# Three small moves in the attention and Fourier phase: tiny copies to GpSimd, later roundings, a priority for a head's low parts

## The chip, the cores and the metric

The kernel runs on one core of one Trainium2 chip. The metric is the time of one execution on the device, in microseconds (us); the core's five instruction streams are TensorE (PE, with its weight loads as PEld), VectorE (DVE), ScalarE (ACT), GpSimd (POOL) and SyncE (SP, which here issues DMAs only). Each engine runs its own instructions in the order in which they stand in its stream, and waits at an instruction until what that needs is there.

## What is computed

The reference chains three parts on four batches of 576 positions and 512 features:

```python
def _attn_ref(q, k, v, f):                       # 4 batches, 8 heads, 576 x 64
    scores = scale * np.matmul(q, k.transpose(0, 1, 3, 2))
    cum = np.cumsum(np.log(np.clip(f, 0.0001, 1.0)), axis=-1)
    decay = cum[:, :, :, None] - cum[:, :, None, :]
    scores = np.where(causal, -1000000000.0, scores + decay)
    ...
    return np.matmul(attn, v)                    # attn: softmax of scores

def _moe_ref(x, w_ch1, w_ch2):
    mixed = np.real(np.fft.fft(np.fft.fft(x, axis=1), axis=2))
    u = x + mixed
    un = (u - mu) / np.sqrt(var + 1e-06)
    return u + np.maximum(un @ w_ch1, 0.0) @ w_ch2

def _moe2_ref(x, w_theta, w_tok_r, w_tok_i, w_ch):
    theta = x @ w_theta
    zr, zi = x * np.cos(theta), x * np.sin(theta)
    y = np.einsum('ts,bsd->btd', w_tok_r, zr) + np.einsum('ts,bsd->btd', w_tok_i, zi)
    u = x + y
    return u + np.maximum(u @ w_ch, 0.0)
```

Products are made in a 32-bit format with fewer mantissa bits. Where that would lose too much, a number is kept as a **high** part (rounded to the format) and a **low** part (what the rounding left), and both are multiplied.

## The kernel before

**Three phases.** The first, up to about 280 us, does the attention of 32 heads, one after the other, and between their instructions the Fourier transform of each batch as soon as its heads are there. The second (to about 730 us) normalises and applies the two wide matrices of `_moe_ref`; the third is `_moe2_ref`. In the second phase from its first blocks on, and in the third, the order is written out; in the first the program hands its pieces to a scheduler, which orders each engine's stream by a priority (the order in which the pieces are written) and by its own estimate of when operands are ready. What it estimates is not measured; what it puts in a row stays in that row on the chip.

**A head** (`prep_units`, `score_units`). `raw` holds a head's keys and queries, twice over on the two halves of the partitions. ScalarE rounds all of it into `hi` (L205) and copies the rounded queries into `q2` (L207; `q_99` and `q_100` by the head's parity). GpSimd makes the two low parts: of the queries into the lower half of `hi` (L209), of the keys into `kl` (L211), which the pair of heads shares and two further rows of which come from a DMA that GpSimd issues (L186). Five blocks of scores follow, 576 (in two pieces of 448 and 128), 512, 384, 256 and 128 columns wide: for each a product of the high parts (L230, which needs L205 and L209) and one with `kl` and `q2` (L231, which needs L207 and L211). VectorE scales and masks a block, finds its extreme and frees its bank (L239, tiles `P` and `mn`), ScalarE takes the exponential (L244), TensorE transposes (L269), VectorE and ScalarE fetch the result (L272, `PT`), TensorE multiplies by the values (L301). `wide` (L250, GpSimd) holds the reciprocal row sums, spread over a diagonal.

**A batch's Fourier transform** (`evac_pair`, `fft_units`). A pair of heads ends in the tile `X`, its mirror in `Y` (L327). GpSimd adds and subtracts them into `E` and `O` (L347, L350). `fft_units` then folds the time axis: `ee` from `E` (L379) and `oo` from `O` (L383), 128x574 elements each, on `two`, which is GpSimd for the first three batches and VectorE for the last. The two columns of `ee` that are their own mirror are copied by ScalarE (L380, 4 elements in a partition), which then rounds `ee` into `eh` (L381) and `oo` into `oh` (L384); the low parts `el` (L386) and `ol` (L388) go to `two`. TensorE's first transform reads `eh` and `el` (L408), `oh` and `ol` (L419). The same is done for a single row, `xx` (L372, its copy L373, `xh` L374, `xl` L375).

Three times, for the first three batches, this folding falls between two heads: near 100, 168 and 232 us. The text below calls these places **hole 0, hole 1 and hole 2**.

Of the kernel before, what the change touches and what calls it, by code (L numbers as in the profile page):

```python
# [13 lines left out]
ALU = mybir.AluOpType  # L14
# [37 lines left out]
def f(ap):  # L52
    return ap.bitcast(F32)


class Net:
    def __init__(self, ctx, tc, ins, out):
        self.ctx, self.tc, self.nc = ctx, tc, tc.nc
        self.i, self.out = ins, out
        nc = self.nc  # L60
        self.base = ctx.enter_context(tc.tile_pool(name="base", bufs=1))
        self.psa = ctx.enter_context(tc.tile_pool(name="psa", bufs=3, space=PSUM))
        self.psb = ctx.enter_context(tc.tile_pool(name="psb", bufs=3, space=PSUM))
        self.pt = ExitStack()
        self.pst = self.pt.enter_context(tc.tile_pool(name="pst", bufs=1, space=PSUM))
        self.nout = 0
        self.u = self.base.tile([128, 4, B * S], F32, name="u")
        self.ident = self.base.tile([128, 128], F32, name="ident")
        self.mean = self.base.tile([128, 128], F32, name="mean")
        nc.gpsimd.memset(self.mean, 1.0 / 512.0)  # L70
        self.eps = self.base.tile([128, 1], F32, name="eps")
        nc.gpsimd.memset(self.eps, 1e-6)
        self.un = {}
        self.stash = {}
        self.sdram = ctx.enter_context(tc.tile_pool(name="sdram", bufs=1, space=DRAM))

    def bank_a(self):
        return self.psa.tile([128, 512], F32, tag="a", name="pa")
# [116 lines left out]
    def prep_units(self, n, pair, raw, hd):  # L195
        nc = self.nc
        g = n % 2
        kl, q2 = pair["kl"], self.q2[g]
        hi = self.w2.tile([128, 2, S], F32R, tag="hi", name="hi")
        hd["hi"] = hi  # L200
        if n == 0:
            nc.scalar.copy(hi[:, 1], raw[:, 1])
            nc.scalar.copy(hi[:, 0], raw[:, 0])
        else:
            nc.scalar.copy(hi, raw)  # L205
        yield
        nc.scalar.copy(q2[0:64], raw[0:64, 1])  # L207
        lows = nc.vector if n == 0 else nc.gpsimd
        lows.tensor_tensor(hi[64:128, 1], raw[64:128, 1], f(hi[64:128, 1]), ALU.subtract)  # L209
        yield  # L210
        lows.tensor_tensor(kl[0:64, g], raw[0:64, 0], f(hi[0:64, 0]), ALU.subtract)  # L211
        yield

    def score_units(self, hd, g):
# [139 lines left out]
    def fft_units(self, b, E, O, rows):  # L354
        nc = self.nc
        w = self.c1
        x256 = self.x256
# [4 lines left out]
        two = nc.vector if b == B - 1 else nc.gpsimd  # L362
        ee = w.tile([128, 2, 290], F32, tag="ee", name="ee", bufs=1)
        oo = w.tile([128, 2, 288], F32, tag="oo", name="oo", bufs=1)
        xx = w.tile([1, 290], F32, tag="xx", name="xx", bufs=1)
        eh = w.tile([128, 2, 290], F32R, tag="eh", name="eh", bufs=1)
        el = w.tile([128, 2, 290], F32R, tag="el", name="el", bufs=1)
        oh = w.tile([128, 2, 288], F32R, tag="oh", name="oh", bufs=1)
# [1 line left out]
        xh, xl = self.xh, self.xl  # L370
        nc.gpsimd.memset(xx[:, 288:290], 0.0)
        nc.gpsimd.tensor_tensor(xx[:, 1:288], x256[:, 1:288], x256[:, 575:288:-1], ALU.add)  # L372
        nc.scalar.copy(xx[:, 0:289:288], x256[:, 0:289:288])  # L373
        nc.scalar.copy(xh[0:1], xx)  # L374
        nc.gpsimd.tensor_tensor(xl[0:1], xx, f(xh[0:1]), ALU.subtract)  # L375
        nc.gpsimd.memset(ee[:, :, 288:290], 0.0)
        nc.gpsimd.memset(oo[:, :, 286:288], 0.0)
        yield
        two.tensor_tensor(ee[:, :, 1:288], E[:, :, 1:288], E[:, :, 575:288:-1], ALU.add)  # L379
        nc.scalar.copy(ee[:, :, 0:289:288], E[:, :, 0:289:288])  # L380
        nc.scalar.copy(eh, ee)  # L381
        yield
        two.tensor_tensor(oo[:, :, 0:287], O[:, :, 1:288], O[:, :, 575:288:-1], ALU.subtract)  # L383
        nc.scalar.copy(oh, oo)  # L384
        yield
        two.tensor_tensor(el, ee, f(eh), ALU.subtract)  # L386
        yield
        two.tensor_tensor(ol, oo, f(oh), ALU.subtract)  # L388
        for _ in range(4):
# [799 lines left out]
```

## Time and profile before

| what | value |
|---|---|
| time, median of 3 runs | 970.92 us (970.60 to 971.12) |
| the profiled execution's own time | 972.97 us |
| its span | 971.2 us |
| TensorE busy in it | 906.7 us (93%) |
| ScalarE, GpSimd busy | 430.9 us, 337.4 us |

The span goes from the first to the last instruction that the profiler recorded; 1.8 us of the execution lie outside it. The profiled execution took 2.05 us more than the median of the runs. In every row of the trace the time at which an idle period ended stands with the instruction that began then, in brackets, with what released it. "Granted clock" is the clock that TensorE was given, as a share of the full 2.4 GHz; 0.50 is 1.2 GHz.

### The profile page before, as it was taken

To read this page: it belongs to the slowest core of one execution; us is meant where nothing else is said; L and a number is where in the kernel's file an instruction comes from. 1 tells how busy PE (TensorE), PEld (TensorE's weight loads), DVE (VectorE), ACT (ScalarE), POOL (GpSimd) and SP (SyncE) were. 2 spreads that over 40 slices of the span, in tenths; PEclk is the share of its full clock that TensorE was granted. 3 is DMA by queue.
4 is the path that set the end of the run, shared out by engine and by line. 5 is a ranking of instruction groups with operands and counts; after the bars stand their busy time and mean duration, and the time that the engine had idled before them with its cause. 6 is when DMAs were issued, how large, how long until landed. Compare 5 with 4: busy or idle time off the path is not lost.

```text
span 971.2 us, 15852 instructions
## 1 busy us (share of the span) xinstructions
PE 906.7 (93%) x5960; PEld 849.4 (87%) x5960; DVE 605.8 (62%) x1469; ACT 430.9 (44%) x1037; POOL 337.4 (35%) x381
## 2 busy tenths in 40 slices
PE   4899898997969999999999999999999999999998
PEld 3677676775748889999999999999999999999998
DVE  7666466474589796544765466536677765746554
ACT  5888677677553443212332222212334534525331
POOL 5776678677540334200000000000024644525330
PEclk9999899997999899999999999999999999999999
DMA  4643232222022121002214022333420000010001
GB/s 145 201 139 119 87 101 89 91 76 88 15 92 83 45 87 44 2 4 84 75 57 159 25 79 86 112 109 114 129 61 1 1 25 25 2 37 14 25 26 49
DMA packets 24336, 68.04 MB, mean 70 GB/s; under 512 B 3534, under 2 KB 6990, under 8 KB 24260
## 3 DMA queue, kind: packets, MB, share of 16 engines
q1 hardware_dynamic: 20420, 62.52, 19.9%
q0 software_dynamic: 3120, 3.33, 1.4%
q10 hardware_dynamic: 720, 1.18, 0.4%
q8 instruction: 47, 0.77, 0.3%
q14 instruction: 29, 0.24, 0.1%
HBM read 57.92 MB, written 9.07 MB: 69 GB/s over the span
## 4 chain that ended last, share of the span: by engine, by line
PE 58%; DVE 10%; ACT 3%; DMA 2%; issue 1%; POOL 1%; ACTq 0%; DVEq 0%; SPq 0%; POOLq 0%
PE pa L747 18%; PE pb L761 11%; PE po L761 8%; PE pb L968 5%; PE pa L979 4%; PE pa L932 4%; PE po L968 3%; DMA raw<-in_wf 1%; DVE kra L939 1%; DVE kra L956 1%; DVE kra L942 1%; DVE a L567 1%; DVE a L565 1%; PE pb L431 1%; DVE kra L941 1%
## 5 line engine op out<-in xcount | busy, mean ns | idle before, releaser
L747 PE MATMUL pa<-un,wf 128*128 128x384 f32 x1152 | 222.5, 341 | 5.3 <-ACT un L735 3.1
L747 PEld LDWEIGHTS pa<-un,wf 128*128 128x128 f32 x1152 | 204.1, 191 | 8.9 <-ACT un L735 4.2
L753 DVE SCALAR_TENSOR_TENSOR h<-pa,h 128x384 fp32r<-128x384 f32 x96 | 53.1, 556 | 145.0 <-ACT h L752 144.8
L761 PE MATMUL pb<-h,wf 128*128 128x384 f32 x660 | 134.9, 337 | 0.3 <-DVE u L769 0.3
L761 PEld LDWEIGHTS pb<-h,wf 128*128 128x128 f32 x660 | 116.6, 188 | 1.2 <-DVE u L769 1.0
L752 ACT ACTIVATE h<-pa 128x384 fp32r<-128x384 f32 x96 | 46.6, 489 | 151.6 <-PE pa L747 151.6
L244 ACT ACTIVATE P<-P,mn 128x512 f32<-128x512 f32 (+4 forms) x160 | 95.5, 600 | 37.7 <-DVE mn L239 37.3
L239 DVE CUSTOM_DVE_ANT_0 P<-pa,mask 128x448 f32<-128x448 f32 (+4 forms) x160 | 77.5, 510 | 51.9 <-PE pa L231 43.9
L761 PE MATMUL po<-h,wf 128*128 128x384 f32 x492 | 104.2, 340 | 1.6 <-DVE h L753 0.7
L924 POOL COPY xd<-u 128x64 f32<-128x64 f32 x32 | 6.7, 253 | 272.4 <-DVE u L769 264.1
L968 PE MATMUL pb<-wtk,z 128*128 128x288 f32 x513 | 97.0, 294 | 0.0
L230 PE MATMUL pa<-hi 128*128 128x448 f32 (+2 forms) x192 | 70.8, 386 | 24.3 <-ACT hi L205 11.0
L761 PEld LDWEIGHTS po<-h,wf 128*128 128x128 f32 x492 | 87.6, 190 | 3.4 <-DVE h L753 1.0
L269 PE MATMUL pb<-ident,P 128*128 128x128 f32 x480 | 82.8, 285 | 5.7 <-ACT PT L272 2.1
L958 POOL TENSOR_TENSOR z<-kra,z 128x256 fp32r<-128x256 f32 x72 | 53.8, 766 | 86.9 <-ACT z L957 86.9
L968 PEld LDWEIGHTS pb<-wtk,z 128*128 128x128 f32 x513 | 79.2, 188 | 0.0
L968 PE MATMUL po<-wtk,z 128*128 128x288 f32 x351 | 75.1, 295 | 1.1 <-POOL z L958 1.1
L231 PE MATMUL pa<-kl,q 66*128 66x448 f32 (+2 forms) x192 | 64.1, 362 | 8.5 <-POOL kl L211 4.3
L269 PEld LDWEIGHTS pb<-ident,P 128*128 128x128 f32 x480 | 57.8, 145 | 11.8 <-issue 2.7
L230 PEld LDWEIGHTS pa<-hi 128*128 128x128 f32 x192 | 38.0, 203 | 33.1 <-issue 11.9
L932 PE MATMUL pa<-wf,xs 128*128 128x256 f32 x456 | 63.9, 289 | 0.0
L209 POOL TENSOR_TENSOR hi<-raw,hi 64x576 fp32r<-64x576 f32 x31 | 44.1, 1424 | 43.7 <-ACT hi L205 25.3
(207 smaller groups left out, 1697.2 us busy)
## 6 DMA issues: line engine op xcount, KB each, us to landing
raw<-in_qk SPq DMA_DIRECT2D x31, 576.0 KB, 3.8
raw<-in_wf SPq DMA_DIRECT2D x32, 512.0 KB, 3.7
raw<-in_wtk SPq DMA_DIRECT2D x18, 288.0 KB, 2.8
v<-in_vp SPq DMA_DIRECT2D x16, 320.0 KB, 3.5
out<-ob SPq DMA_DIRECT2D x12, 288.0 KB, 2.1
dft<-in_dft POOLq DMA_DIRECT2D x8, 346.0 KB, 6.1
raw<-in_wth SPq DMA_DIRECT2D x4, 512.0 KB, 3.6
st_wth<-raw SPq DMA_DIRECT2D x4, 512.0 KB
```

What stands on the lines that cost most here:

```text
L230: nc.tensor.matmul(t[:, 0 : b - a], hi[:, 1, q], hi[:, 0, a:b], start=True, stop=False)
L231: nc.tensor.matmul(t[:, 0 : b - a], q2[:, q], kl[:, g, a:b], start=False, stop=True)
L239: nc.vector.tensor_tensor_reduce(out=p[:, a:b], in0=t[:, 0 : b - a], in1=self.mask[:, S - n0 - 128 + a : S - n0 - 128 + b], scale=-0.125, ...
L244: nc.scalar.activation(p, p, AF.Exp, bias=lowest, scale=-1.0, accum_out=zs[:, g, i : i + 1])
L269: nc.tensor.transpose(ps[:, o : o + 128], src, self.ident)
L747: nc.tensor.matmul(ps[:, 0:CH], t[:, l, 128 * d : 128 * d + 128], un[r][:, d], start=n == 0, stop=n == 11)
L752: nc.scalar.activation(h[:, 0], ps[:, 0:CH], AF.Relu)
L753: nc.vector.scalar_tensor_tensor(h[:, 1], ps[:, 0:CH], 0.0, f(h[:, 0]), ALU.max, ALU.subtract)
L761: nc.tensor.matmul(outs[d], t[:, l, 128 * d : 128 * d + 128], h[:, r], start=k % G == 0 and n == 0, stop=k % G == G - 1 and n == 2,)
L932: nc.tensor.matmul(th, xs[:, l, d], self.wth[d][:, r, 256 * hf : 256 * hf + 256], start=n == 0, stop=n == 11)
L958: nc.gpsimd.tensor_tensor(z[:, 1], t, f(z[:, 0]), ALU.subtract)
L968: nc.tensor.matmul(acc[k][th], z[:, l, 128 * k : 128 * k + 128], self.wtk[kt][:, r, 288 * th : 288 * th + 288], start=first and i == 0 and ...
```

## The change

Four edits, all in the first phase. Line numbers of the changed kernel are some ten higher (L209 is L218 there, L211 L221, L207 L215, L250 L260, L244 L254, L380 L389, L379 L390, L383 L392, L381 L394, L386 L396, L384 L397, L388 L399).

1. The copies of the two unmirrored columns (`xx`, `ee`) go from ScalarE to GpSimd; for `ee` to `two`, ahead of the addition.
2. `behind` gives the scheduler an order without a semaphore: the rounding `eh` is not put in the row before the subtraction `oo` is, and `oh` not before the low part `el` is. On the chip nothing waits for these.
3. A head's query copy (L207) and its two low parts (L209, L211) get a priority of 60 places.
4. One more `yield` in `fft_units`, so that its pieces are handed over in smaller portions.

```diff
+    def behind(self, ins, other):
+        self.tc.add_manual_dep(
+            ins.ins, other.ins.name,
+            mybir.DependencyInfo(mybir.DependencyClass.NoSync, mybir.DependencyReason.DATA),
+            reason="behind",
+        )
...
-        nc.scalar.copy(q2[0:64], raw[0:64, 1])
+        with self.tc.high_priority(60):
+            nc.scalar.copy(q2[0:64], raw[0:64, 1])
         lows = nc.vector if n == 0 else nc.gpsimd
-        lows.tensor_tensor(hi[64:128, 1], raw[64:128, 1], f(hi[64:128, 1]), ALU.subtract)
-        yield
-        lows.tensor_tensor(kl[0:64, g], raw[0:64, 0], f(hi[0:64, 0]), ALU.subtract)
+        with self.tc.high_priority(60):
+            lows.tensor_tensor(hi[64:128, 1], raw[64:128, 1], f(hi[64:128, 1]), ALU.subtract)
+        yield
+        with self.tc.high_priority(60):
+            lows.tensor_tensor(kl[0:64, g], raw[0:64, 0], f(hi[0:64, 0]), ALU.subtract)
         yield
...
-        nc.scalar.copy(xx[:, 0:289:288], x256[:, 0:289:288])
+        nc.gpsimd.tensor_copy(xx[:, 0:289:288], x256[:, 0:289:288])
...
+        two.tensor_copy(ee[:, :, 0:289:288], E[:, :, 0:289:288])
         two.tensor_tensor(ee[:, :, 1:288], E[:, :, 1:288], E[:, :, 575:288:-1], ALU.add)
-        nc.scalar.copy(ee[:, :, 0:289:288], E[:, :, 0:289:288])
-        nc.scalar.copy(eh, ee)
-        yield
-        two.tensor_tensor(oo[:, :, 0:287], O[:, :, 1:288], O[:, :, 575:288:-1], ALU.subtract)
-        nc.scalar.copy(oh, oo)
-        yield
-        two.tensor_tensor(el, ee, f(eh), ALU.subtract)
+        yield
+        odd = two.tensor_tensor(oo[:, :, 0:287], O[:, :, 1:288], O[:, :, 575:288:-1], ALU.subtract)
+        yield
+        self.behind(nc.scalar.copy(eh, ee), odd)
+        yield
+        low = two.tensor_tensor(el, ee, f(eh), ALU.subtract)
+        self.behind(nc.scalar.copy(oh, oo), low)
         yield
         two.tensor_tensor(ol, oo, f(oh), ALU.subtract)
```

**GpSimd, around the first pair of batch 0** (near 70 us; `E` and `O` are the pair's sum and difference, L209 and L211 the next head's low parts). Before:

```order
L338 MEMSET Y 1x576
L209 TENSOR_TENSOR hi<-raw,hi 64x576
L347 TENSOR_TENSOR E<-X,Y 128x576
L350 TENSOR_TENSOR O<-X,Y 128x576
L211 TENSOR_TENSOR kl<-raw,hi 64x576
```

and after:

```order
L218 TENSOR_TENSOR hi<-raw,hi 64x576
L348 MEMSET Y 1x576
L221 TENSOR_TENSOR kl<-raw,hi 64x576
L357 TENSOR_TENSOR E<-X,Y 128x576
L360 TENSOR_TENSOR O<-X,Y 128x576
```

The key's low part stands ahead of the pair's sum and difference instead of behind them.

**GpSimd, hole 0** (from the low parts of the head that TensorE turns to next). Before:

```order
L209 TENSOR_TENSOR hi<-raw,hi 64x576
L211 TENSOR_TENSOR kl<-raw,hi 64x576
L250 TENSOR_SCALAR wide<-rz_98 128x640
L347 TENSOR_TENSOR E<-X,Y 128x576
L350 TENSOR_TENSOR O<-X,Y 128x576
L379 TENSOR_TENSOR ee<-E 128x2x287
L383 TENSOR_TENSOR oo<-O 128x2x287
L386 TENSOR_TENSOR el<-ee,eh 128x580
L388 TENSOR_TENSOR ol<-oo,oh 128x576
```

and after:

```order
L218 TENSOR_TENSOR hi<-raw,hi 64x576
L221 TENSOR_TENSOR kl<-raw,hi 64x576
L357 TENSOR_TENSOR E<-X,Y 128x576
L360 TENSOR_TENSOR O<-X,Y 128x576
L260 TENSOR_SCALAR wide<-rz_98 128x640
L389 COPY ee<-E 128x2x2
L392 TENSOR_TENSOR oo<-O 128x2x287
L390 TENSOR_TENSOR ee<-E 128x2x287
L396 TENSOR_TENSOR el<-ee,eh 128x580
L399 TENSOR_TENSOR ol<-oo,oh 128x576
```

The copy is new, and `oo` has come to stand ahead of `ee`.

**ScalarE, hole 0** (`q_100` is the query copy of the head whose scores come next, `P` its exponentials and those of the head before). Before:

```order
L244 ACTIVATE P,zs_95<-P,mn 128x384
L244 ACTIVATE P,zs_95<-P,mn 128x256
L380 COPY ee<-E 128x2x2
L207 CAST q_100<-raw 64x576
L381 CAST eh<-ee 128x580
L384 CAST oh<-oo 128x576
L244 ACTIVATE P,zs_95<-P,mn 128x128
```

and after:

```order
L295 COPY R<-pb 128x512
L254 ACTIVATE P,zs_95<-P,mn 128x384
L215 CAST q_99<-raw 64x576
L293 COPY R<-pa 128x64
L394 CAST eh<-ee 128x580
L254 ACTIVATE P,zs_95<-P,mn 128x256
L254 ACTIVATE P,zs_95<-P,mn 128x128
L397 CAST oh<-oo 128x576
```

`q_100` is no longer among these rows: it now stands 13 rows ahead of `eh`, right behind the rounding `hi` of its head; the exponentials of 256 and 128 columns stand behind `eh`, which waits for `ee` as the copy did before.

## Rows read from the trace of the kernel before

**Rows 1.** The page: busy time, share of the span and instructions of each engine.

```profile
PE 906.7 (93%) x5960; PEld 849.4 (87%) x5960; DVE 605.8 (62%) x1469; ACT 430.9 (44%) x1037; POOL 337.4 (35%) x381
```

**Rows 2.** Busy time by stretch: us, then PE, PEld, DVE, ACT, POOL, clock, DMA.

```profile
375.00:425.00 50.00, 50.00 (x297) 49.73 (x296) 22.78 (x44) 13.23 (x26) 12.96 (x14) 1.00 0.04 11
```

**Rows 3.** Waits of PE, 0 to 312 us: us in total, times, longest.

```profile
PE pa L230 <- POOL hi L209: 6.3, 2, 5.3
PE pa L231 <- POOL kl L211: 4.3, 5, 1.4
```

**Rows 4.** Waits of ACT, 0 to 312 us.

```profile
ACT ee L380 <- POOL ee L379: 10.5, 3, 4.1
```

**Rows 5.** Timeline of PE at four short gaps: start, us, instruction, idle before.

```profile
43.17 0.47 PE L230 MATMUL pa<-hi 128*128 128x448 f32 x1 [0.95 <-POOL hi L209]
44.65 0.74 PE L231 MATMUL pa<-kl,q 66*128 66x448 f32 x1 [1.01 <-POOL kl L211]
...
70.99 0.54 PE L231 MATMUL pa<-kl,q 66*128 66x448 f32 x2 [1.42 <-POOL kl L211]
...
202.45 0.47 PE L231 MATMUL pa<-kl,q 66*128 66x448 f32 x1 [0.74 <-POOL kl L211]
...
218.39 0.47 PE L231 MATMUL pa<-kl,q 66*128 66x448 f32 x1 [0.42 <-POOL kl L211]
```

**Rows 6.** Timeline of POOL ahead of the first and the fourth of these gaps.

```profile
40.92 0.71 POOL L250 TENSOR_SCALAR wide<-rz 128x640 f32<-128x640 f32 x1 [0.79 <-ACT hi L205]
...
216.24 0.72 POOL L250 TENSOR_SCALAR wide<-rz 128x640 f32<-128x640 f32 x1
```

**Rows 7.** Busy time by stretch, as in rows 2, behind two short gaps.

```profile
44.00:48.00 4.00, 3.35 (x13) 2.86 (x14) 1.03 (x3) 2.37 (x8) 0.60 (x1) 0.58 0.47 159
72.00:76.00 4.00, 4.00 (x22) 2.61 (x22) 2.12 (x7) 3.60 (x8) 1.54 (x2) 0.58 0.42 145
```

**Rows 8.** Timelines of hole 0: POOL, then ACT, then PE.

```profile
96.64 0.72 POOL L250 TENSOR_SCALAR wide<-rz 128x640 f32<-128x640 f32 x1
...
100.06 1.39 POOL L379 TENSOR_TENSOR ee<-E 128x574 f32<-128x574 f32 x1
```

```profile
101.49 0.20 ACT L380 COPY ee<-E 128x4 f32<-128x4 f32 x1 [3.56 <-POOL ee L379]
102.16 0.67 ACT L381 CAST eh<-ee 128x580 fp32r<-128x580 f32 x1
```

```profile
102.40 1.15 PE L231 MATMUL pa<-kl,q 66*128 66x448 f32 x3 [3.92 <-ACT q L207]
...
106.69 3.56 PE L301 MATMUL pt<-PT,v 128*64 128x256 f32 x18
```

**Rows 9.** Timeline of PE in holes 1 and 2.

```profile
167.81 0.69 PE L230 MATMUL pa<-hi 128*128 128x384 f32 x1 [2.60 <-DVE mn L239]
...
170.61 0.69 PE L269 MATMUL pb<-ident,P 128*128 128x128 f32 x2 [1.58 <-ACT PT L272]
...
234.83 0.85 PE L230 MATMUL pa<-hi 128*128 128x448 f32 x2 [5.35 <-POOL hi L209]
...
241.35 3.07 PE L301 MATMUL pt<-PT,v 128*64 128x256 f32 x20
```

**Rows 10.** Line L379: durations in ns, least, median and most; and POOL's smallest copies.

```profile
L379 POOL TENSOR_TENSOR ee<-E x3: 1392/1393/1393, 100.1 to 229.8; 128x574 f32<-128x574 f32 x3
L379 DVE TENSOR_TENSOR ee<-E x1: 751/751/751, 296.1 to 296.1; 128x574 f32<-128x574 f32 x1
```

```profile
L924 POOL COPY xd<-u 128x64 f32<-128x64 f32 x32 | 6.7, 253 | 272.4 <-DVE u L769 264.1 <-PE pa L928 8.2
```

**Rows 11.** The start: the issue of head 1's `raw` (SP), its landing, the first low part.

```profile
1.57 0.43 SPq L192 DMA_DIRECT2D raw<-in_qk  x1
```

```profile
raw<-in_qk SPq DMA_DIRECT2D x2, 576.0 KB, 3.9
```

```profile
10.11 0.74 DVE L209 TENSOR_TENSOR hi<-raw,hi 64x576 fp32r<-64x576 f32 x1
```

## The prediction

> **What bounds the kernel now.** I read the busy shares first [rows 1]: TensorE is busy for 93% of the span, so a change pays only where TensorE stands still or runs at the lower clock. The busy time by stretch says where that can be: behind phase 1 TensorE is full (50.00 of 50 us at clock 1.00, [rows 2]), and no edit touches code there. What the change can win is thus in the first 290 us. There I read the waits of TensorE, of which the edits address two: for a head's query low part, 6.3 us in 2 waits, 5.3 of it in hole 2, and for its key low part, 4.3 us in 5 waits [rows 3]. Next the waits of ScalarE: it stands still for 10.5 us in three pieces before the tiny copy of `ee`, because that copy needs GpSimd's addition [rows 4], and behind it in the row stand things that TensorE wants. So the three holes are one story: GpSimd folds, ScalarE stands behind it, TensorE runs dry. In hole 0 TensorE waits 3.92 us for a query copy that is ready to run but stands behind the stuck one [rows 8]; in hole 1 it waits 2.60 and 1.58 us, in hole 2 5.35 [rows 9]. Together that is 13.45 us. Lastly the clock: after two of the short gaps it was granted at 0.58 for 4 us [rows 7].
>
> **Short gaps (the priority on the low parts).** Nothing is added; GpSimd's row is permuted. Four gaps, one by one.
> At 43 to 45 us TensorE lost 0.95 and 1.01 us to two low parts [rows 5]. Ahead of them GpSimd did `wide`, which began 0.79 us late because it waited for the row's head [rows 6]; with `wide` behind the low parts they come a good 0.7 us earlier. I take -0.8 (bounds -1.96, the whole of both gaps, and 0).
> At 70.99 us it lost 1.42 us to the key's low part [rows 5], which stood behind two GpSimd operations of 1.39 us each (the same size as the addition in [rows 10]); the order puts it ahead of both. -1.42 (bounds -1.42 and 0).
> At 202.45 us the opposite happens: `wide` now stands ahead of the low parts, so the gap of 0.74 us [rows 5] grows by its 0.72 [rows 6]. +0.72 (bounds 0 and +0.72).
> At 218.39 us `wide` stood between the two low parts [rows 6] and goes; the gap of 0.42 us [rows 5] with it. -0.42.
> Sum: -0.80 - 1.42 + 0.72 - 0.42 = -1.92.
> **The clock.** After the first two gaps TensorE was busy for 3.35 and 4.00 us at 0.58 [rows 7], which cost 0.42 x 3.35 = 1.4 and 0.42 x 4.00 = 1.7 us. The second gap goes whole (-1.7). The first shrinks by under half, so I take half of its 1.4 (-0.7). The gap at 202 grows to 1.46, as long as the one that was followed by the lower clock, so it gets the same price (+1.7). Sum -0.7 (bounds -3.1 and +1.7).
>
> **The copies and the roundings (the holes).** The copy leaves ScalarE, but what it waited for does not: `eh` needs the whole of `ee`, so the wait passes to `eh`. On GpSimd the chain to the end of `ee` has become longer: the copy comes in, priced by the smallest copy there is, 0.25 us [rows 10] (it has fewer elements, so between 0 and 0.25), and `oo` with 1.39 has come ahead of `ee`. That is +1.64 us before `eh` can start.
> Here the notes bear on the choice of engine. The row: the same addition of `ee` takes 1.39 us on GpSimd and 0.75 on VectorE [rows 10]. The Trainium skill, "GPSIMD Engine Reference", section "Engine selection", says that elementwise work belongs on VectorE, about twice as slow on GpSimd with two inputs and near line rate with one; the trace agrees (1.85 times), and by its second half the copy would cost next to nothing beyond its start, which would make the 1.64 a 1.39 plus a little and changes the sum by under 0.2 us a hole.
> Hole 0: `ee` ran at 100.06 and ended at 101.45; now it ends 1.64 later, at 103.1. `eh` began at 102.16 [rows 8], behind the copy and the query copy; it begins at 103.1, +0.95. Against this the query copy is early, so that TensorE has all of the next head's scores to do while it waits, and the 3.92 us gap is filled; but two exponentials now stand behind `eh`, and the transposes that need them stand ahead of the value product L301 (106.69, [rows 8]). By then it will have done about the same work as before, and later. I take the delay of `eh`, +0.95 (bounds -3.92 and +1.64).
> Hole 1: the same chain, +1.64 for `ee`; but here the order puts both late exponentials ahead of `eh`, and the 1.58 us that TensorE waited for a transposed block [rows 9] can go. Nearest to +1.0 for the later rounding with a part of the 1.58 gained: +0.6 (bounds -1.58 and +1.64).
> Hole 2: both low parts stand ahead of `oo` and `ee` now, so TensorE gets its next head near 231.9 rather than 234.83 [rows 9], 2.9 us earlier. What follows, the transform of `eh` and `el`, is later, since two low parts (2.8 us) and the copy came ahead of `ee`; L301 at 241.35 [rows 9] comes near 240.5. -0.9 (bounds -2.9 and +1.64).
> Sum of the holes: +0.95 + 0.6 - 0.9 = +0.65.
> ScalarE's own time falls by two copies of 0.20 us a batch [rows 8]; they hide in its waits, so they count zero.
>
> **The start.** The query copy of head 1 is put ahead of head 0's roundings on ScalarE and so waits for its `raw`. That is issued at 1.57 us and takes 0.43 to issue and 3.9 to land, so it is there near 5.9. Head 0's low part runs on VectorE only at 10.11 [rows 11]. Zero, with 1.5 us as its upper bound should the landing be much later.
>
> **How the numbers follow.** -1.92 - 0.7 + 0.65 = -1.97. The profiled execution took 972.97 us, 2.05 above the median of the runs, so it becomes 971.0, and the median 970.92 becomes 968.95. A measurement of this kernel tells about 0.2% from no change, 1.94 us, so this lies on the very edge of faster.
>
> **Rivals.**
> (a) The holes open. With `q2`, the low parts and the exponentials early, TensorE has scores all through the stall of ScalarE. For it: the wait of 3.92 us is for a copy that needs nothing from GpSimd. Against: later work in the same row still ends at `eh`. Half of the 13.45 us gone and the short gaps with their clock (-2.6) make 970.92 - 6.7 - 2.6 = 961.6.
> (b) Slower: the longer GpSimd chain decides. If TensorE reaches the value product with nothing left to do, each hole ends later by what `ee` is later: 1.64 in holes 0 and 1, and about 3.5 in hole 2, where low parts came ahead too: +6.8. With the short gaps -2.6 this is +4.2, 975.1. It decides as soon as ScalarE reaches `eh` more than 1.64 us before `ee` ends in all three; its waits of 10.5 us in 3 [rows 4] speak for that.
> (c) The change does not do what it says: the low parts wait for the rounding `hi` just ahead of them anyway, and a priority cannot pass that; gaps move by some tenths either way, 970.5.
>
> **Chances.** The forecast, with its own range 966.5 to 970.9, 0.45, of which a bit over half lies beyond 0.2%; (a) 0.20; (b) 0.22; (c) 0.13. Faster by over 0.2%: 0.24 + 0.20 = 0.44. Within: 0.20 + 0.09 = 0.29. Slower: 0.22 + 0.01 from the forecast + 0.04 from (c) = 0.27. The range reaches from the better part of (a) to the better part of (b): 961.5 to 974.5.
>
> **What would show it.** In the changed profile: no wait for the key's low part near 71 us, and clock 1.00 behind it; one of about 1.4 near 202. ScalarE's waits before `ee` are gone and stand before `eh`, 10 to 13 us in 3. On GpSimd `ee` ends some 1.6 us later in hole 0. TensorE's gap in hole 0 for the query copy is gone and another, for transposed blocks, stands a little later. The prediction is wrong if the waits before `eh` sum to under 6 us (a), or if L301 comes over 2 us later in each hole (b), or if the time moves in the second or third phase, where I expect nothing.

## The result: 8 us slower, and the profile after

The changed kernel takes 978.45 us (median of 5 runs, 977.07 to 978.89) against 970.60 of the kernel before on the same chip: a ratio of 1.0079, with a 95% interval of 1.0065 to 1.0094, or +7.7 us where -2 was forecast. Between the two profiled executions the spans differ by 5.9 us (977.1 and 971.2); the profiled one of before is on the slow side of its runs, so traces are compared here for where time goes, and times for how much. One execution on record, of the kernel e_lowonly2 below, took 1817.78 us and is left out of its figures.

Busy time on the page of after, as in [rows 1]:

```profile
PE 911.7 (93%) x5960; PEld 852.1 (87%) x5960; DVE 609.0 (62%) x1470; ACT 430.2 (44%) x1029; POOL 339.1 (35%) x388
```

TensorE does the same 5960 matmuls and is busy 5 us longer, so the clock has a part in the loss. Summed over stretches of 4 us from 0 to 440 us, TensorE stands still for 56.7 us before and 57.1 after, and loses 18.1 and 23.0 us to the clock (busy time times one minus the granted clock). Between these two profiled executions nearly the whole difference is thus clock; the waits matter by what follows them. To see where, I lined the traces up by work: each matmul counts with the shortest duration that its shape has in either trace, and the lag is how much later the changed kernel has done what the kernel before had done at a time.

| time in the trace of before (us) | 24 | 36 | 48 | 78 | 96 | 114 | 132 | 162 | 180 | 222 | 252 | 276 | 300 | 348 | 414 |
|---|---|---|---|---|---|---|---|---|---|---|---|---|---|---|---|
| lag of after (us) | -1.4 | 5.5 | 2.2 | 1.7 | 4.8 | 4.7 | 3.8 | 7.2 | 6.8 | 6.2 | 7.9 | 6.4 | 9.9 | 5.5 | 5.7 |

Hole 0 lies between 96 and 114, hole 1 between 162 and 180, hole 2 between 222 and 252. The first two cost nothing here and the third 1.7; most of the loss comes up between the holes, at 24 to 36, 78 to 96 and 132 to 162. Of what comes up at 24 to 36, more than half is won back by 78, where the kernel before has its own gaps of [rows 5]. At the end of the first phase (276 to 300) another 3.5 us come up, and early in the second 4.4 are won back. The clock goes the same way there: from 280 to 312 us it costs 2.0 us before and 5.9 after, from 312 to 440 us 4.6 before and 1.4 after. Which wait starts this was not followed.

Waits of TensorE in after, 0 to 312 us (total, times, longest), beside [rows 3]:

```profile
PE pb L279 <- ACT P L254: 6.5, 5, 2.1
PE pa L241 <- POOL kl L221: 5.1, 6, 1.0
PE pa L240 <- POOL hi L218: 3.6, 4, 2.2
```

and of ScalarE, beside [rows 4]:

```profile
ACT eh L394 <- POOL ee L390: 13.2, 3, 5.1
```

The low parts that were to stop holding TensorE up still do: the key's for 5.1 us in 6 waits instead of 4.3 in 5, the query's for 3.6 in 4 instead of 6.3 in 2 (the longest, in hole 2, is down from 5.35 to 2.18). They do it at other places. Timeline of TensorE in after (start, us, instruction, idle before), beside [rows 5]:

```profile
27.41 0.53 PE L240 MATMUL pa<-hi 128*128 128x448 f32 x2 [0.62 <-POOL hi L218]
28.89 0.54 PE L241 MATMUL pa<-kl,q 66*128 66x448 f32 x2 [0.94 <-POOL kl L221]
...
81.32 0.47 PE L240 MATMUL pa<-hi 128*128 128x448 f32 x1 [0.45 <-POOL hi L218]
82.79 0.47 PE L241 MATMUL pa<-kl,q 66*128 66x448 f32 x1 [0.99 <-POOL kl L221]
...
140.87 0.47 PE L241 MATMUL pa<-kl,q 66*128 66x448 f32 x1 [1.00 <-POOL kl L221]
...
155.44 0.47 PE L240 MATMUL pa<-hi 128*128 128x448 f32 x1 [0.32 <-POOL hi L218]
156.93 0.47 PE L241 MATMUL pa<-kl,q 66*128 66x448 f32 x1 [1.01 <-POOL kl L221]
```

Behind the first two pairs the clock fell. Busy time by stretch (us, PE, PEld, DVE, ACT, POOL, clock, DMA), after:

```profile
28.00:32.00 4.00, 3.11 (x10) 2.24 (x10) 2.69 (x10) 0.61 (x1) 3.85 (x4) 0.66 0.55 179
32.00:36.00 4.00, 4.00 (x14) 3.52 (x14) 3.04 (x13) 3.77 (x13) 3.35 (x5) 0.50 0.79 223
36.00:40.00 4.00, 4.00 (x22) 3.12 (x22) 2.25 (x8) 2.77 (x9) 0.58 (x1) 0.56 1.00 257
...
84.00:88.00 4.00, 4.00 (x20) 3.63 (x19) 3.09 (x12) 2.47 (x6) 2.34 (x3) 0.59 0.67 226
```

and before, where these stretches had the whole clock:

```profile
32.00:36.00 4.00, 4.00 (x32) 3.00 (x28) 2.35 (x13) 2.84 (x8) 3.93 (x6) 1.00 0.70 212
```

Fourteen matmuls where there were 32, in the same 4 us of busy time. In after, the four stretches lose (1 - 0.66) x 3.11 + 0.50 x 4 + 0.44 x 4 + 0.41 x 4 = 6.4 us to the clock; the two of [rows 7] that are gone had cost 3.1.

Why the low parts came late near 27 us is told by ScalarE's row. After:

```profile
17.96 0.66 ACT L215 CAST q<-raw 64x576 fp32r<-64x576 f32 x1
...
21.96 0.67 ACT L215 CAST q<-raw 64x576 fp32r<-64x576 f32 x1 [1.10 <-PE pa L241]
...
24.73 1.14 ACT L212 CAST hi<-raw 128x1152 fp32r<-128x1152 f32 x1
```

and before:

```profile
23.17 1.14 ACT L205 CAST hi<-raw 128x1152 fp32r<-128x1152 f32 x1
...
25.21 0.66 ACT L207 CAST q<-raw 64x576 fp32r<-64x576 f32 x1
```

The priority lifted two heads' query copies over the rounding `hi` of the first of these heads. The second of them even waited 1.10 us, because TensorE was still reading the old `q2`. The rounding, which has no priority, slid from 23.17 to 24.73, and GpSimd could start the low parts only at its end: their query part came at 25.95 instead of 24.39. After, then before:

```profile
25.95 1.41 POOL L218 TENSOR_TENSOR hi<-raw,hi 64x576 fp32r<-64x576 f32 x1 [1.92 <-ACT hi L212]
```

```profile
24.39 1.41 POOL L209 TENSOR_TENSOR hi<-raw,hi 64x576 fp32r<-64x576 f32 x1
```

Ahead of the pair near 82 us it is the same: two query copies, at 72.92 and 76.25 us, stand ahead of the rounding of the first of their heads. After, then before:

```profile
78.56 1.16 ACT L212 CAST hi<-raw 128x1152 fp32r<-128x1152 f32 x1
```

```profile
73.09 1.16 ACT L205 CAST hi<-raw 128x1152 fp32r<-128x1152 f32 x1
```

Near 140 and 156 us the copy is not the whole reason. Ahead of the wait at 140.87 GpSimd has the pair's `E` and `O` and both output additions in a row, and is done with them no earlier than ScalarE with the rounding:

```profile
136.45 1.17 ACT L212 CAST hi<-raw 128x1152 fp32r<-128x1152 f32 x1
```

```profile
136.40 1.44 POOL L460 TENSOR_TENSOR u<-ea,oa 128x576 f32<-128x576 f32 x1
137.92 1.42 POOL L218 TENSOR_TENSOR hi<-raw,hi 64x576 fp32r<-64x576 f32 x1
```

Ahead of 155.44 the rounding is done at 152.76 us, and GpSimd's own row (output additions and zeroing of tiles) lasts till 153.90. The head is the one that waited 0.74 us at 151.09 before.

### The profile page after: what moved, and what is told of

It is laid out like the page before. It is cut to its first block, busy times and chain, and to the rows that moved or that the text cites. A ratio compares the mean times of both kernels' runs of the same rounds, so it can differ in the third digit from the quotient of the medians.

```text
span 977.1 us, 15853 instructions
## 1 busy us (share of the span) xinstructions
PE 911.7 (93%) x5960; PEld 852.1 (87%) x5960; DVE 609.0 (62%) x1470; ACT 430.2 (44%) x1029; POOL 339.1 (35%) x388
## 3 DMA queue, kind: packets, MB, share of 16 engines
q1 hardware_dynamic: 20420, 62.52, 19.8%
## 4 chain that ended last, share of the span: by engine, by line
PE 67%; DVE 10%; ACT 6%; POOL 5%; issue 2%; DMA 0%; ACTq 0%; POOLq 0%; DVEq 0%; SPq 0%
PE pa L758 18%; PE pb L772 11%; PE po L772 8%; PE pb L979 5%; PE pa L990 4%; PE pa L943 4%; PE pt L311 4%; PE po L979 3%; PE pb L442 2%; ACT P L254 2%; PE pb L279 2%; PE pb L419 1%; DVE kra L953 1%; DVE kra L950 1%; DVE kra L967 1%
## 5 line engine op out<-in xcount | busy, mean ns | idle before, releaser
L254 ACT ACTIVATE P<-P,mn 128x512 f32<-128x512 f32 (+4 forms) x160 | 95.7, 600 | 38.9 <-DVE mn L249 38.4
L240 PE MATMUL pa<-hi 128*128 128x448 f32 (+2 forms) x192 | 74.0, 395 | 20.4 <-DVE hi L218 11.3
L241 PE MATMUL pa<-kl,q 66*128 66x448 f32 (+2 forms) x192 | 67.2, 372 | 5.1 <-POOL kl L221 5.1
L218 POOL TENSOR_TENSOR hi<-raw,hi 64x576 fp32r<-64x576 f32 x31 | 43.8, 1413 | 50.8 <-ACT hi L212 30.0
```

Source lines behind the costliest of these rows:

```text
L240: nc.tensor.matmul(t[:, 0 : b - a], hi[:, 1, q], hi[:, 0, a:b], start=True, stop=False)
L241: nc.tensor.matmul(t[:, 0 : b - a], q2[:, q], kl[:, g, a:b], start=False, stop=True)
L254: nc.scalar.activation(p, p, AF.Exp, bias=lowest, scale=-1.0, accum_out=zs[:, g, i : i + 1])
```

## The experiments

Each row is a kernel that keeps only some of the parts, measured beside the kernel before on the same chip, 4 to 12 times; differences are the measured ratio's distance from 1 times 970 us. The medians as they stand differ from that by about 1 us or less, except for e_qonly (+15.2 by medians) and e_hiprio (+4.8). Differences of 2 us between two rows are within the intervals.

| kernel | parts | against before (us) | 95% interval of the ratio |
|---|---|---|---|
| changed | all | +7.7 | 1.0065 to 1.0094 |
| e_noprio | copies, roundings, yield | +19.8 | 1.0168 to 1.0241 |
| e_prioonly | priority on query copy and low parts | +9.4 | 1.0065 to 1.0129 |
| e_qprio | copies, roundings, yield, priority on query copy | +12.6 | 1.0099 to 1.0161 |
| e_lowprio | copies, roundings, yield, priority on low parts | +5.4 | 1.0035 to 1.0077 |
| e_yield | extra yield | +15.2 | 1.0134 to 1.0179 |
| e_copies | copies | +3.0 | 1.0019 to 1.0043 |
| e_behind | roundings | +0.8 | 0.9991 to 1.0024 |
| e_less | all but the yield | +11.3 | 1.0095 to 1.0139 |
| e_lowonly | priority on low parts | -2.4 | 0.9957 to 0.9993 |
| e_lowonly2 | the same again | -1.2 | 0.9973 to 1.0003 |
| e_qonly | priority on query copy | +17.3 | 1.0148 to 1.0207 |
| e_hiprio | all, and priority on the rounding | +6.2 | 1.0042 to 1.0086 |
| e_hi_low | priority on rounding and low parts | +0.3 | 0.9989 to 1.0017 |
| e_yield_low | yield, priority on low parts | +3.2 | 1.0013 to 1.0054 |
| e_q_hi_low | priority on query copy, rounding, low parts | +4.8 | 1.0028 to 1.0071 |
| e_low_behind | priority on low parts, roundings | -1.6 | 0.9967 to 1.0000 |

**First question: the priority or the folding?** Theory A held the priority for the culprit, theory B the longer chain on GpSimd (copy and `oo` ahead of `ee`). e_noprio takes the priority off:

```diff
-        with self.tc.high_priority(60):
-            nc.scalar.copy(q2[0:64], raw[0:64, 1])
+        nc.scalar.copy(q2[0:64], raw[0:64, 1])
...
-        with self.tc.high_priority(60):
-            lows.tensor_tensor(kl[0:64, g], raw[0:64, 0], f(hi[0:64, 0]), ALU.subtract)
+        lows.tensor_tensor(kl[0:64, g], raw[0:64, 0], f(hi[0:64, 0]), ALU.subtract)
```

> The changed kernel without any priority: only the copies on GpSimd, the roundings behind GpSimd's operations and the extra yield. Theory A (the priority costs the time: query copies ahead on ScalarE push a head's rounding and with it the low parts later): about as before, -2 to +2 us. Theory B (the folding chain on GpSimd costs it, oo ahead of ee and the copy ahead of both): most of the loss stays, +5 to +8 us, with ScalarE waiting 13 us before eh.

It was +19.8: neither theory. A is down as told, and B foresaw a loss but not one that is more than twice that of the whole change. Its lag is under 1 us until 132 us, all through hole 0, and jumps by 7.6 between 132 and 138, where no folding is near (and by 7.9 between 199 and 208). e_prioonly is the other half, the same three lines with the priority in the kernel before:

> The kernel before with the priority of 60 on query copy and low parts and nothing else. Theory A: +5 to +8 us against before, with new waits of TensorE for the key's low part near 28 us and a clock of about 0.5 behind it. Theory B: -3 to 0 us.

+9.4: a loss as A had it, if above its 5 to 8, with the waits near 28 us and the clock of 0.50 behind them. So each half loses by itself, and together they lose no more than the smaller one: the priority takes back much of what the other edits lose. Splitting it (e_qprio keeps the priority on L207's copy only, e_lowprio on L209's and L211's subtractions only):

> The changed kernel with the priority on the query copy alone, none on the low parts. Theory A (the query copy is what pushes the roundings back): +5 to +8 us. If the low parts' priority is what costs: 0 to +2 us. Theory B: +5 to +8 us.

> The changed kernel with the priority on the low parts alone, none on the query copy. Theory A: -2 to +2 us against before. If the low parts' priority is what costs: +5 to +8 us. Theory B: +5 to +8 us.

With the low parts first the loss falls from 19.8 to 5.4, with the query copy first only to 12.6. Both lie outside what A gave: taking the priority off the query copy leaves 5.4 of the 7.7, so that priority is not the whole loss of the change.

**Second question: which of the folding edits?** The place of the jump pointed at the smallest one, the extra `yield` that the prediction had not costed (theory C). e_yield has nothing else:

```diff
         nc.scalar.copy(eh, ee)
         yield
+        yield
         two.tensor_tensor(oo[:, :, 0:287], O[:, :, 1:288], O[:, :, 575:288:-1], ALU.subtract)
```

> The kernel before with nothing but the extra yield behind the piece that makes ee and eh: the Fourier pieces that follow are handed over one round later. Theory C (the yield slips E, O and the output additions on GpSimd ahead of the next head's low parts; what cost 20 us in the changed kernel without priority): +14 to +21 us, with TensorE waiting over 4 us for a query low part near 140 us and the lower clock behind. Theory B (copies and roundings do it): -1 to +2 us.

+15.2 us for one empty yield. (It stands ahead of `oo` here and behind it in the changed kernel; in both all that follows from `el` on comes one round later.) GpSimd in e_yield, timeline:

```profile
129.01 1.41 POOL L449 TENSOR_TENSOR u<-ea,oa 128x576 f32<-128x576 f32 x1
130.40 1.42 POOL L347 TENSOR_TENSOR E<-X,Y 128x576 f32<-128x576 f32 x1
131.78 1.42 POOL L350 TENSOR_TENSOR O<-X,Y 128x576 f32<-128x576 f32 x1
133.17 1.40 POOL L450 TENSOR_TENSOR u<-ea,oa 128x576 f32<-128x576 f32 x1
134.56 0.72 POOL L250 TENSOR_SCALAR wide<-rz 128x640 f32<-128x640 f32 x1
135.36 1.40 POOL L209 TENSOR_TENSOR hi<-raw,hi 64x576 fp32r<-64x576 f32 x1
```

and in the kernel before:

```profile
132.16 1.41 POOL L449 TENSOR_TENSOR u<-ea,oa 128x576 f32<-128x576 f32 x1
133.65 1.41 POOL L209 TENSOR_TENSOR hi<-raw,hi 64x576 fp32r<-64x576 f32 x1
```

Before, `E` and `O` had begun at 126.04 and 127.40, ahead of the output additions and of a wait. One round later they fall together: sum, difference, both output additions `u` and `wide`, 6.4 us in a row, stand ahead of the head's low parts, although ScalarE was done with that head's rounding at 129.18. TensorE and its clock (1.00 before) behind that, in e_yield:

```profile
136.81 0.52 PE L230 MATMUL pa<-hi 128*128 128x448 f32 x1 [3.48 <-POOL hi L209]
...
211.05 0.85 PE L230 MATMUL pa<-hi 128*128 128x448 f32 x2 [4.48 <-POOL hi L209]
```

```profile
136.00:140.00 4.00, 2.45 (x9) 1.95 (x10) 0.79 (x3) 1.43 (x2) 3.07 (x3) 0.64 0.20 32
140.00:144.00 4.00, 4.00 (x20) 2.71 (x21) 0.20 (x2) 1.43 (x3) 1.90 (x2) 0.51 0.54 207
```

The same row of GpSimd comes again near 204 us with the wait of 4.48 us behind it. The lag of e_yield against before rises by some 7 us at each of the two places: most of the 15. The other two edits by themselves. e_copies:

```diff
-        nc.scalar.copy(xx[:, 0:289:288], x256[:, 0:289:288])
+        nc.gpsimd.tensor_copy(xx[:, 0:289:288], x256[:, 0:289:288])
...
+        two.tensor_copy(ee[:, :, 0:289:288], E[:, :, 0:289:288])
         two.tensor_tensor(ee[:, :, 1:288], E[:, :, 1:288], E[:, :, 575:288:-1], ALU.add)
-        nc.scalar.copy(ee[:, :, 0:289:288], E[:, :, 0:289:288])
```

> The kernel before with the tiny copies on GpSimd and nothing else. Theory C: -1 to +2 us. Theory B: +3 to +10 us.

and e_behind, with as many yields as before:

```diff
-        nc.scalar.copy(eh, ee)
         yield
-        two.tensor_tensor(oo[:, :, 0:287], O[:, :, 1:288], O[:, :, 575:288:-1], ALU.subtract)
-        nc.scalar.copy(oh, oo)
+        odd = two.tensor_tensor(oo[:, :, 0:287], O[:, :, 1:288], O[:, :, 575:288:-1], ALU.subtract)
+        self.behind(nc.scalar.copy(eh, ee), odd)
         yield
-        two.tensor_tensor(el, ee, f(eh), ALU.subtract)
+        low = two.tensor_tensor(el, ee, f(eh), ALU.subtract)
+        self.behind(nc.scalar.copy(oh, oo), low)
```

> The kernel before with the roundings behind GpSimd's operations and nothing else (copies on ScalarE, as many yields as before). The order of GpSimd is unchanged by it, TensorE's and ScalarE's in a few rows. Theory C: -2 to +1 us. Theory B: +3 to +10 us.

The roundings cost nothing that can be measured. The copies cost 3.0 us, more than C allowed, and the trace shows 2.6 of it in hole 0: from 96 to 116 us TensorE stands still for 6.5 us instead of 4.9 and loses 3.8 to the clock instead of 2.8. In place of the 3.92 us for the query copy [rows 8] it waits for `eh`:

```profile
102.18 0.80 PE L408 MATMUL pb<-dft,eh 128*128 128x258 f32 x2 [5.26 <-ACT eh L381]
```

Later the lag shrinks again; the profiled execution of e_copies (973.16 us) is one of its fastest, so its span of 971.4 does not show the 3.0. GpSimd's row in e_copies has the copy at 98.52, `oo` at 98.66 and `ee` at 100.02: it is this edit, and neither the roundings nor the yield, that puts `oo` ahead of `ee`, so e_copies has the whole of theory B's longer chain. Yield, copies and roundings by themselves sum to 15.2 + 3.0 + 0.8 = 19.0, and e_noprio, which has all three, is at +19.8. And the changed kernel without the yield,

```diff
         odd = two.tensor_tensor(oo[:, :, 0:287], O[:, :, 1:288], O[:, :, 575:288:-1], ALU.subtract)
-        yield
         self.behind(nc.scalar.copy(eh, ee), odd)
```

> The changed kernel without its extra yield. Theory C with the yield as the only culprit: -3 to +1 us against before. If the priority costs by itself, as its run alone says: +5 to +10 us.

is at +11.3, slower than with it. So what the yield costs depends on what else stands there; theory C with the yield as the only culprit is down too, and the priority's own cost stands.

**Third question: what in the priority costs?** Theory D: the query copy. Theory E: the low parts too. In the kernel before, e_lowonly puts it on the low parts,

```diff
-        lows.tensor_tensor(hi[64:128, 1], raw[64:128, 1], f(hi[64:128, 1]), ALU.subtract)
+        with self.tc.high_priority(60):
+            lows.tensor_tensor(hi[64:128, 1], raw[64:128, 1], f(hi[64:128, 1]), ALU.subtract)
         yield
-        lows.tensor_tensor(kl[0:64, g], raw[0:64, 0], f(hi[0:64, 0]), ALU.subtract)
+        with self.tc.high_priority(60):
+            lows.tensor_tensor(kl[0:64, g], raw[0:64, 0], f(hi[0:64, 0]), ALU.subtract)
```

> The kernel before with the priority on the two low parts alone. Theory D (the query copy's priority is what costs in the priority's own +9.5 us: it puts the copies of both heads ahead of a head's rounding on ScalarE, the rounding and so the low parts come late, TensorE waits and the clock falls): -3 to +1 us. Theory E (the low parts' priority costs too, because it moves other GpSimd work behind them): +4 to +9 us.

and e_qonly on the query copy:

```diff
-        nc.scalar.copy(q2[0:64], raw[0:64, 1])
+        with self.tc.high_priority(60):
+            nc.scalar.copy(q2[0:64], raw[0:64, 1])
```

> The kernel before with the priority on the query copy alone. Theory D: +7 to +13 us, with the low-part waits near 28 us and a clock of 0.5 to 0.66 from 28 to 40 us. Theory E: 0 to +3 us.

-2.4 and +17.3: D, although it gave e_qonly 7 to 13 only; E is down in both. e_qonly has the same lower clock that the changed kernel has:

```profile
28.00:32.00 4.00, 3.11 (x11) 2.67 (x12) 2.26 (x10) 1.16 (x3) 3.81 (x5) 0.60 0.55 179
32.00:36.00 4.00, 3.67 (x12) 2.84 (x12) 2.40 (x11) 3.18 (x11) 3.46 (x4) 0.50 0.64 189
36.00:40.00 4.00, 4.00 (x24) 3.26 (x25) 2.65 (x10) 3.50 (x13) 0.58 (x1) 0.62 1.01 292
```

If the copy costs because it passes a rounding, a priority on the rounding must give it back. On the changed kernel:

```diff
         else:
-            nc.scalar.copy(hi, raw)
+            with self.tc.high_priority(60):
+                nc.scalar.copy(hi, raw)
```

> The changed kernel with the same priority on the rounding of a head as well, so that it is not passed by its own and the next query copy. Theory D: 3 to 7 us less than the changed kernel, so +1 to +5 us against before, and no low-part waits near 28 us. Theory E: as the changed kernel, +7 to +10 us.

The clock there is whole again (the stretches as above, in e_hiprio), and TensorE's waits for GpSimd's low parts shrink from 8.7 us to one of 0.4:

```profile
28.00:32.00 4.00, 4.00 (x26) 3.70 (x25) 3.14 (x15) 3.27 (x14) 2.47 (x5) 1.00 0.88 257
32.00:36.00 4.00, 3.50 (x25) 2.81 (x24) 3.89 (x17) 4.00 (x11) 3.14 (x3) 1.00 0.66 163
```

```profile
PE pa L242 <- POOL kl L222: 0.4, 1, 0.4
```

But the time is only 1.5 us less than that of the changed kernel (+6.2 against +7.7; 3.0 by medians; the intervals overlap), at best the lower end of the 3 to 7 that D promised. Other waits took the place: up to 312 us TensorE still stands still for 52.3 us, after 53.2 in the changed kernel, among them

```profile
PE pb L420 <- ACT R L296: 4.1, 1, 4.1
```

So passing the rounding explains the waits near 28 us and the clock behind them, and not the whole +7.7. The same lines, with those of e_lowonly (e_hi_low) and with those of e_qonly as well (e_q_hi_low), on the kernel before:

> The kernel before with the priority on the rounding and the low parts, none on the query copy: a try at what the priority was for. Theory D: -5 to 0 us. Theory E: +3 to +8 us.

> The kernel before with the priority on query copy, rounding and low parts alike. If the query copy costs because it passes the rounding: -3 to +3 us, against +9.5 without the priority on the rounding. If it costs by itself (ScalarE waits for the query buffer): +6 to +10 us.

+0.3 and +4.8, the second between the two ranges given. The priority on the rounding thus gives back about half of e_prioonly's 9.4. The rest comes with the query copy's priority (+4.8 with it, +0.3 without); by which wait is open.

**Last: do the parts explain the whole?** The yield of e_yield and the lines of e_lowonly together, in the kernel before:

> The kernel before with the extra yield and the priority on the low parts. If that priority takes back what the yield loses (it lifts the query low part over the sum, the difference and the two output additions, the key low part over the two additions only): +1 to +6 us, and TensorE's wait near 137 us under 2 us. If the two add up: +11 to +14 us.

+3.2, where 15.2 and -2.4 would add to +13. The low parts' priority takes back most of the yield's loss, and not all: with low parts first the yield still costs some 4 to 6 us (+3.2 against -2.4 and -1.2). The wait near 137 us is down to the key's (the profiled execution, 967.87 us, was the kernel's fastest):

```profile
134.10 0.47 PE L233 MATMUL pa<-kl,q 66*128 66x448 f32 x1 [1.95 <-POOL kl L213]
```

With this the table has two ways from the kernel before to the changed one. Low parts first, then yield, then copies and roundings, then the query copy: -2.4, +3.2, +5.4, +7.7. Or the whole priority first, then copies and roundings, then the yield: +9.4, +11.3, +7.7. On the first way the yield is the dearest step and the query copy's priority adds 2.3, on the second the priority is the dearest and the yield gives back 3.6. No part has a share of the 7.7 of its own.

Two tries for a faster kernel, e_lowonly measured again and e_low_behind, which adds the two `behind` lines:

> The kernel before with the priority on the two low parts alone, measured again: -4 to -1 us if the gain of 2.4 us is one, -1 to +1 us if it was chance.

> The kernel before with the priority on the low parts and the roundings behind GpSimd's operations; copies, yields and query copy as before. Parts add: -2.4 + 0.8, so -4 to 0 us.

-1.2 and -1.6: the three measurements of kernels with the low parts first and nothing else that costs are all under before, between 0.1% and 0.25%, and all 9 to 10 us under the changed kernel. That they beat the kernel before is likely, not certain: the upper ends of the intervals are 0.9993, 1.0003 and 1.0000.

## Why the prediction was wrong, point by point

What failed is two terms of the sum that were put at nothing: what the priority on the query copy does to the rounding that it passes (+17.3 us alone, e_qonly), and the extra yield (+15.2 alone, e_yield). The sum went by the gaps that the trace of before had, and the changed order made others. The low parts' priority, the one term that was costed as a gain, is one (-2.4 and -1.2 alone, where -1.92 and the clock's -0.7 stood).

- **What bounds the kernel**: right for the third phase and most of the second. From 414 us on nothing moves (the lag stays 5.7 to 5.9). But the loss comes up between the holes rather than in them, and time moves where nothing was expected to: early in the second phase 4.4 us of lag go, with the clock.
- **Short gaps**: wrong, and the first failing step. The working went through the gaps that were there (all but the one of 0.74 us at 151.09) and asked which would go. At 71 us and 218 us they went as said, and at 43 to 45 us 0.66 was left of 1.96; the one at 202 us did not grow but went. But six new ones came up, and the one at 151.09 grew to 1.01. Four of the six, near 28 and 82 us, came because the query copy's priority was costed only at the start and where TensorE waited for that copy, and not at what it passes in ScalarE's row later; the two at 140.87 and 155.44 stand behind GpSimd's own row. All short waits for low parts outside the holes sum to 0.62 + 0.94 + 0.66 + 0.45 + 0.99 + 1.00 + 0.32 + 1.01 = 5.99 us in after, against 0.95 + 1.01 + 1.42 + 0.74 + 0.74 + 0.42 = 5.28 before: +0.7, where -1.92 stood.
- **The clock**: wrong with it, and the larger part. -0.7 stood; 6.4 us were lost in the four stretches shown against 3.1 before, +3.3. In and behind the holes the clock costs 9.2 us instead of 8.4, from 280 to 440 us 7.3 instead of 6.6; for these two no term stood.
- **The yield**: left out of the sum, although named as an edit. Alone it costs 15.2 us. That the changed kernel does not lose that is mostly the low parts' priority (e_yield_low, +3.2), which the prediction had seen only as a gap filler. With these the yield still costs 4 to 6 us.
- **The holes**: right as a picture. `ee` began at 105.80 in hole 0, behind `oo` and a copy of 0.18 us (bounds 0 to 0.25), and ScalarE's wait passed to `eh`, 13.2 us in 3 waits, where 10 to 13 were expected:

```profile
104.28 0.18 POOL L389 COPY ee<-E 128x4 f32<-128x4 f32 x1
104.43 1.40 POOL L392 TENSOR_TENSOR oo<-O 128x574 f32<-128x574 f32 x1
105.80 1.40 POOL L390 TENSOR_TENSOR ee<-E 128x574 f32<-128x574 f32 x1
```

  TensorE stood for exponentials behind `eh`, as said:

```profile
108.46 1.12 PE L279 MATMUL pb<-ident,P 128*128 128x128 f32 x4 [1.71 <-ACT P L254]
110.48 0.90 PE L279 MATMUL pb<-ident,P 128*128 128x128 f32 x3 [0.91 <-ACT PT L282]
111.45 3.15 PE L311 MATMUL pt<-PT,v 128*64 128x256 f32 x14
```

  By the lag hole 0 cost -0.1 (said +0.95), hole 1 -0.4 (+0.6), hole 2 +1.7 (-0.9): together +1.2 for +0.65, near only because the misses cancel. Why hole 2 came out the other way was not followed.
- **The start**: the price was nearly right, the landing was not. The copy of head 1's queries waited till 7.05 us, not 5.9, and pushed the first rounding from 5.59 to 8.45; TensorE began at 11.28 instead of 11.00:

```profile
7.05 0.67 ACT L215 CAST q<-raw 64x576 fp32r<-64x576 f32 x1 [2.28 <-DMA raw<-in_qk]
...
8.45 0.67 ACT L209 CAST hi<-raw 128x576 fp32r<-128x576 f32 x1
```

- **The rival (b)** came out on the right side (975.1, slower) for the wrong reason. It had +6.8 for the longer chain in the holes; e_copies, which has all of that chain, costs 3.0, and in the changed kernel the holes cost 1.2 by the lag.
- **The engine for the copies**: the Trainium skill, "GPSIMD Engine Reference", section "Engine selection", says that elementwise work is about twice as slow there with two inputs and near line rate with one. The trace agrees for two inputs (1.39 us against 0.75, [rows 10]); the copy of 4 elements in a partition took 0.18 us, against 0.20 for ScalarE's in [rows 8], which is too small to show a rate.

## What to carry to other kernels

A priority on one instruction is a demotion of all that it passes: before it is costed at nothing, look at what stood between its old place and its new one on its own engine, and who waits for that; here it was the rounding from which the low parts are made. Where a scheduler orders the program by rounds, an empty yield is an edit like any other: it shifts a whole train of work, and what counts is which instructions then fall together on one engine ahead of one that TensorE waits for. And single edits of one change need not add: measure the parts one by one and at least the pairs that touch the same engine.

## What the runs showed that was not expected

Behind the waits of 0.62 and 0.94 us near 28 us (two more, 0.54 and 0.78 us, lie just ahead of them) some 10 us went by at clocks of 0.50 to 0.66 (28 to 40 us, after and e_qonly): about 4.8 us lost behind 2.9 us of waits. Two other pairs in after are nearly alike: 0.45 and 0.99 us near 82 us, 0.32 and 1.01 us near 156 us. The first was followed by 4 us at 0.59, the second by the whole clock. So of two pairs of like size one can be followed by a loss longer than itself and the other by none; what decides, these runs do not show.
